# Half-width stationary values in the first attention stage of a fused attention and ELU feed-forward kernel

## The chip, the core and the metric

The kernel runs on one core of a Trainium2 chip. The metric is device time in microseconds (us). A core has TensorE (PE: matrix products into PSUM), VectorE (DVE), ScalarE (ACT), GpSimd (POOL) and SyncE (SP), which issues the DMAs. The engines run side by side, each through its own list of instructions in a fixed order, and wait for each other on semaphores.

## The reference

Eight batches of eight heads with 576 tokens and a head dimension of 64 go through causal attention with a decay bias, and the result, 4608 tokens of 512 values, through a feed-forward layer of 2048 with an ELU-like step between.

```python
scores = scale * np.matmul(q, k.transpose(0, 1, 3, 2))
cum = np.cumsum(np.maximum(s, 0.0), axis=-1)
bias = -(cum[:, :, :, None] - cum[:, :, None, :])
scores = np.where(causal, -1000000000.0, scores + np.minimum(bias, 0.0))
attn = np.exp(scores - np.max(scores, axis=-1, keepdims=True))
attn = attn / (np.sum(attn, axis=-1, keepdims=True) + 1e-09)
x = np.matmul(attn, v)            # then (B, S, H * D) as (4608, 512)
h = x @ w_in
g = np.where(h > 0.0, h, np.exp(np.minimum(h, 0.0)) - 1.0)
out = g @ w_out
```

## The kernel before, in words

The program first records operations (`op`), each with its engine or engines to choose from, an assumed cost, the tiles that it reads and writes, and a priority. `Plan.issue` then plays them through and writes them out: at each step it takes the operation that can start first by the assumed costs, so a changed cost or a changed operation may move anything that comes later, and may put a step on another engine. The instructions of an engine then run in exactly that order.

The attention is cut in two stages. The first stage (`Low`) takes the first 320 rows of batches 0, 1 and 2, twelve units of one batch and one pair of heads each, and works in plain fp32. The second stage (`Unit`) takes all the rest, in f16 parts. The feed-forward layer goes over 12 chunks of 384 tokens; chunk 0 runs in fp32 (`hidden_native`, L1313, and its `project`, L1358), the others in f16 parts (L1329, L1366). Chunk 0 needs the first stage's results of batches 0 and 1 and runs between its last units. Up to 60 us of the plan, PE gets filler transposes (L1429) where it would idle.

A unit of the first stage goes like this:

- `prepare_low` loads keys and queries of both heads (`kl`, `ql`) and the values (`vs`, two buffers in turn), and takes the largest magnitude of the values (`peak`, L579). The loaded block has seven slots of 64 columns: slot 0 with the first 64 keys' values of both heads, one above the other in the partitions, then for key blocks 0, 1 and 2 one slot for each head. `vs` keeps each slot with 64 columns of zeros beside it, so the DMA writes seven pieces a partition, 64 columns each and 128 apart. The zeros are written once, by four memsets in `zeros` (L511, L512).
- `scoring_low` makes the scores (L981), the masked row minimum (L984), exp (L989) and the normalized probabilities (L1002, L1004, L1006): one block for the pair's first 64 rows, and for each head blocks of 192 and 320 keys.
- `weighing_low` turns the probabilities with PE transposes (L793, L807) into `trl`, copies them to `tl` in SBUF (L417 on ACT or L418 on DVE), and multiplies with the values into one PSUM bank, `avl` (L788). `av` has one buffer, so a unit's first product waits until the last unit's results have been copied out.

The products are the step that changes. `own(k)` is a window of 128 stationary columns: a head's 64 value columns and 64 zeros, to the right of them for the first head and to the left for the second. So every product writes all 128 partitions of the bank; head 0 adds its values to partitions 0 to 63 and zeros to 64 to 127, head 1 the other way round. Key block 0 has 256 moving columns a head, block 1 has 192, block 2 has 64, and the pair's product has 128: seven fp32 products a unit, 84 in all. They accumulate in one group from the first (block 0, head 0, `start`) to the last (block 2, head 1, `stop`). Each is an operation of its own with the assumed cost `pe4(c)`.

The second stage's products (`heads`, L1143) already use 64 stationary columns a head, in f16, the two heads in turn, each into its own half of the bank's partitions.

Of the kernel before, what the change touches and what calls it, by code (L numbers as in the profile page):

```python
# [9 lines left out]
F32 = mybir.dt.float32  # L10
# [7 lines left out]
P = 128  # L18
# [25 lines left out]
N_CUT, CUT = 3, 2  # L44
# [241 lines left out]
def pe4(n):  # L286

    return 4 * pe(n)
# [41 lines left out]
def kernel(  # L330
# [26 lines left out]
    D = vb.shape[4]  # L357
    NP = H // 2
# [3 lines left out]
    HB = P // 2  # L362
    NQ = (S - HB) // P
# [4 lines left out]
    const = ctx.enter_context(tc.tile_pool(name="const", bufs=1))  # L368
# [8 lines left out]
    def load(prio, dst, src, reads, writes, nbytes, late=(), lag=LAG):  # L377
        return op(prio, [("SP", SP_COST, lambda: nc.sync.dma_start(dst(), src()), lag, nbytes)],
                  reads, writes, late)
# [53 lines left out]
    WM = S - P  # L433
    LOW = HB + CUT * P

    vs = [plan.buf(const, [P, NQ, 4, D], F32, f"vs_{k}") for k in range(2)]
    maskw = plan.buf(const, [P, WM], BF16, "maskw")
    masks = plan.buf(const, [P, 2, HB], BF16, "masks")

# [60 lines left out]
    def ones():  # L500

        for q, k in ((q2s, k2s), *zip(q2, k2)):
# [2 lines left out]
                pool.memset(k.v[HB:].bitcast(F32), 0.0)  # L505

            op(20, [("Pool-M", 700.0, rows)], [], [(q, "ones"), (k, ("aux", 0)), (k, ("aux", 1))])

    def zeros():
        for v in vs:  # L510
            op(-8, [("Pool-M", 450.0, lambda v=v: pool.memset(v.v[:, :, 3], 0.0))], [], [(v, "zeros")])  # L511
            op(-8, [("Pool-M", 100.0, lambda v=v: pool.memset(v.v[:, 0, 1], 0.0))], [], [(v, 1)])  # L512

    def mask_tiles():
        def whole():
# [191 lines left out]
    def prepare_low(u):  # L707

        b, j, prio = u.b, u.j, u.prio
        u.vs = vs[u.turn]  # L710
        u.k, clear = (k_first, None) if (b, j) == (0, 0) else low_keys(u.tag)
        u.q = plan.buf(sb, [P, 2 * LOW], F32, f"ql_{u.tag}", tag="qs", bufs=2)
        heads, h0 = slice(2 * j, 2 * j + 2), b * H + 2 * j
        at = slice(HB, HB + 1)
        load(prio, lambda: u.k.v[:HB], lambda: kT[b, :HB, heads, :LOW], [], [(u.k, "k")], P * LOW * 4)
        load(prio, lambda: u.q.v[:HB], lambda: qT[b, j, :HB, : 2 * LOW], [], [(u.q, "q")], P * LOW * 4)
        op(prio if b or j else -10, [("Pool-M", pool_1(2 * LOW), lambda: pool.memset(u.q.v[HB:], 1.0))],
           [], [(u.q, "ones")])
        if (b, j) > (0, 0):
            op(prio, clear, [], [(u.k, "sums")])  # L720

            src = aux if (b, j) == (0, 1) else aux_dram
            o = load(prio, lambda: u.k.v[at],
                     lambda: src.v[h0 : h0 + 2, 0, :LOW],
                     [(src, 0)], [(u.k, "sums")], 2 * LOW * 4)
        if (b, j) == (0, 1):
            urgent.append(o)
        n = 1 + 2 * (1 + CUT)

        def values():  # L730
            v = u.vs.v.rearrange("p n a d -> p (n a d)")[:, : n * P]
            return v.rearrange("p (n t d) -> p n t d", t=2, d=D)[:, :, 0]


        load(prio, values, lambda: vb[b, j, :, :n], [], [(u.vs, 0), (u.vs, 2)], P * n * D * 4)
        peak(prio, n * D, values, [(u.vs, 0), (u.vs, 2)], A_LOW + b * NP + j, mybir.AxisListType.XY)

    def scoring_low(u):
        prio = u.prio
# [37 lines left out]
    def weighing_low(u):  # L777
# [3 lines left out]
        av = plan.buf(ps, [P, 512], F32, f"avl_{u.tag}", tag="av", bufs=N_AV)  # L781
        ends = [P]

        def own(k):
            return u.vs.v.rearrange("p n a d -> p (n a d)")[:, k * HB : k * HB + P]

        def product(cost, k, src, dst, start, stop, reads):
            op(prio, [("PE", cost, lambda: pe_.matmul(av.v[:, dst], own(k), src(), start=start, stop=stop))],  # L788
               reads + [u.vs], [av])

        def pair():
            tr = plan.buf(ps, [P, 512], F32, f"trl_{u.tag}", tag="a", bufs=N_A)
            op(prio, [("PE", 111.0, lambda: pe_.transpose(tr.v[:, :P], u.first.v, ident))], [u.first], [tr])  # L793
            psum_copy(prio, P, lambda: turned.v[:, :P], lambda: tr.v[:, :P], [tr], [(turned, "pair")])
            product(pe4(P), 0, lambda: turned.v[:, :P], slice(n, n + P), True, True, [(turned, "pair")])

        def keys(kb):

# [14 lines left out]
            def dst():  # L813
                return turned.v[:, at : at + 2 * c].rearrange("p (h q) -> p h q", h=2)
# [1 line left out]
            psum_copy(prio, 2 * c, dst,  # L816
                      lambda: tr.v[:, : 2 * m * P].rearrange("p (h q) -> p h q", h=2)[:, :, m * P - c :],
                      [tr], [(turned, kb)])
            for h in range(2):
                product(pe4(c), 2 + 4 * kb + h, lambda h=h: dst()[:, h], slice(n - c, n),  # L820
                        kb == 0 and h == 0, kb == CUT and h == 1, [(turned, kb)])
            if kb < CUT:
                return
            key = u.b, u.j, False
# [606 lines left out]

    fillers()
    decay_sums()
    zeros()
    mask_tiles()
    for i in range(NQ):
        zero_pad(-9, pp[i], i)
# [99 lines left out]
```

## Time and profile before

| | |
|---|---|
| median of 3 runs | 1068.13 us (1066.83 to 1070.27) |
| the profiled execution | 1074.05 us |
| its span, from the first to the last instruction | 1072.3 us |
| busy PE / DVE / ACT / POOL | 1027.8 / 864.2 / 644.9 / 421.2 us |
| products of the first stage (L788) | 168 records, 16.9 to 105.3 us |
| products of the second stage (L1143) | 896 records, 147.4 to 938.3 us |

PE in the profile is the stream of products; PEld is the loading of stationary operands, which runs beside it. A group's busy time counts overlaps of its own instructions once. A product's recorded length goes from its start to the modelled end of its results, and the next one starts before that; what a product costs PE is the distance to the next start. An fp32 product shows as two records.

### The profile page before, as it was taken

Reading aid. Unit: us, or ns where it says so; the run is one execution under the profiler, and the core shown is the slowest. Engines: PE = TensorE matmul, PEld = TensorE weight load, DVE = VectorE, ACT = ScalarE, POOL = GpSimd, SP = SyncE. Lnnn points to the kernel's source line nnn. Section 1 sums busy time; section 2 is a strip of 40 time slices with the busy share of each in tenths; the row PEclk is TensorE's granted clock in tenths of the full one; section 3 lists DMA queues with packets and bytes.
Section 4 is the critical chain, followed back from the end, with each engine's and each line's share of the span. In section 5 each row is a group of like instructions: output and inputs, shape, how many; then the busy total and the mean of one; then the engine's idle time right before and its main releaser. Section 6 shows DMA issues by size and latency. Waiting matters only on the chain. (4 is left out here: it accounts for less than half of the span.)

```text
span 1072.3 us, 19689 instructions
## 1 busy us (share of the span) xinstructions
PE 1027.8 (96%) x6007; PEld 614.3 (57%) x6007; DVE 864.2 (81%) x2234; ACT 644.9 (60%) x1521; POOL 421.2 (39%) x649
## 2 busy tenths in 40 slices
PE   8889999899999999999999999999999999999998
PEld 7777555455555555555555555555555555555554
DVE  7788999999978988999898889898988888733433
ACT  5778675556666656566666666665566555544443
POOL 5532335433353445545543545444434534100000
PEclk9999999999999999999999999999999999999999
DMA  6788895536577666675577576757676557320000
GB/s 191 187 240 236 208 225 159 151 85 145 134 178 173 148 157 152 158 183 142 132 183 183 130 192 145 199 150 168 157 169 146 138 148 145 76 65 1 30 1 30
DMA packets 304313, 156.52 MB, mean 146 GB/s; under 512 B 224952, under 2 KB 278992, under 8 KB 304208
## 3 DMA queue, kind: packets, MB, share of 16 engines
q1 hardware_dynamic: 304208, 155.27, 59.2%
q8 instruction: 48, 0.79, 0.3%
q14 instruction: 57, 0.47, 0.1%
HBM read 79.66 MB, written 19.32 MB: 92 GB/s over the span
## 5 line engine op out<-in xcount | busy, mean ns | idle before, releaser
L1329 PE MATMUL h<-xh,wp 128*128 128x384 f16 x1408 | 392.7, 327 | 13.4 <-DVE gg L1347 11.7
L1366 PE MATMUL o<-wp,gg 128*128 128x512 f16 x1584 | 387.5, 380 | 0.0
L1329 PEld LDWEIGHTS <-wp 128*128 128x128 f16 x2112 | 197.2, 98 | 164.2 <-issue 23.4
L1366 PEld LDWEIGHTS <-gg 128*128 128x128 f16 x1584 | 146.4, 98 | 152.8 <-issue 5.4
L1329 PE MATMUL h<-xl,wp 128*128 128x384 f16 x704 | 229.6, 326 | 1.0 <-DVE xl L1282 0.9
L1293 ACT ACTIVATE g<-h,cs 128x384 f32<-128x384 f32 x176 | 101.8, 579 | 152.6 <-PE h L1329 150.7
L1042 DVE SCALAR_TENSOR_TENSOR p<-p,sm,p 128x512 f16<-128x512 f32 (+3 forms) x248 | 173.5, 723 | 7.3 <-POOL p L1034 5.3
L989 ACT ACTIVATE p<-p,mn 128x192 f32<-128x192 f32 (+1 forms) x232 | 144.0, 621 | 56.0 <-DVE mn L984 53.0
L1338 DVE SCALAR_TENSOR_TENSOR h<-g,cs,h 128x384 f32<-128x384 f32 x176 | 108.5, 616 | 74.7 <-ACT g L1300 73.4
L1034 POOL TENSOR_SCALAR p<-p,sm 128x512 f16<-128x512 f32 (+3 forms) x125 | 81.4, 658 | 137.2 <-DVE sm L995 42.0
L1342 ACT ACTIVATE gg<-h 128x384 f16<-128x384 f32 x160 | 78.0, 488 | 88.8 <-DVE h L1338 86.7
L981 PE MATMUL sc<-kh,qs 128*128 128x192 f32 (+2 forms) x272 | 118.8, 439 | 9.1 <-DVE mn L984 8.8
L984 DVE CUSTOM_DVE_ANT_0 p<-sc,maskw 128x192 f32<-128x192 f32 (+1 forms) x232 | 109.1, 480 | 15.8 <-PE sc L981 11.2
L1347 DVE SCALAR_TENSOR_TENSOR gg<-h,gg 128x384 f16<-128x384 f32 x176 | 97.1, 552 | 24.6 <-ACT gg L1342 22.6
L981 PE MATMUL sc<-k,q 128*128 128x192 f32 (+2 forms) x272 | 83.8, 311 | 0.2 <-DMA q<-qs 0.2
L981 PEld LDWEIGHTS sc<-kh,qs 128*128 128x128 f32 x272 | 51.7, 190 | 37.3 <-DVE mn L984 16.0
L1300 ACT ACTIVATE g<-g 128x384 f32<-128x384 f32 x132 | 68.9, 522 | 3.6
L411 POOL TENSOR_TENSOR k<-stk,kh 64x576 fp32r<-64x576 f32 x41 | 61.8, 1508 | 19.1 <-ACT kh L392 13.6
L1038 ACT ACTIVATE p<-p,sm 128x512 f16<-128x512 f32 (+3 forms) x98 | 56.7, 597 | 11.3 <-DVE sm L995 3.7
L1143 PE MATMUL av<-T,v 128*64 128x256 f16 (+5 forms) x896 | 61.0, 286 | 0.0
L1143 PEld LDWEIGHTS <-v 128*64 128x64 f16 x896 | 45.8, 110 | 23.0 <-issue 10.3
L402 POOL TENSOR_SCALAR xh<-xc,cs 128x384 f16<-128x384 f32 x32 | 21.6, 681 | 95.0 <-PE h L1329 89.7
(175 smaller groups left out, 1441.6 us busy)
## 6 DMA issues: line engine op xcount, KB each, us to landing
stk<-in_kT_dram SPq DMA_DIRECT2D x64, 288.0 KB
va<-in_vb_dram SPq DMA_DIRECT2D x32, 320.0 KB
stq<-in_qT_dram SPq DMA_DIRECT2D x40, 256.0 KB
w_i<-in_w_in_dram SPq DMA_DIRECT2D x16, 512.0 KB
w_o<-in_w_out_dram SPq DMA_DIRECT2D x16, 512.0 KB
out_dram<-ost SPq DMA_DIRECT2D x32, 256.0 KB
x_dram<-x_None SPq DMA_DIRECT2D x20, 288.0 KB
q<-qs SPq DMA_DIRECT2D x40, 128.0 KB
```

The costliest lines, as they stand in the source:

```text
L981: pe_.matmul(view(sc.v[:, :cw]), l, r, start=n == 0, stop=n == len(pairs) - 1)
L984: op(prio, [("DVE", 84 + dve_p(cw), lambda i=i, sc=sc: dve.tensor_tensor_reduce(pt.v[:, i * cw : (i + 1) * cw], sc.v[:, :cw], mv(i * cw, c ...
L989: op(prio, [("ACT", 480 + w / 1.2, lambda: act.activation(pt.v[:, :w], pt.v[:, :w], AF.Exp, bias=mn.v[:, n - 1 : n], scale=-1.0, accum_out ...
L1034: ("Pool", 160 + 1.04 * n, lambda part=part: pool.tensor_scalar(part(t16, 0), own(part), sm.v[:, r], 1.0, ALU.mult, ALU.mult)),
L1042: ("DVE-SB", dve_2(n), lambda part=part: dve.scalar_tensor_tensor(part(t16, 1), own(part), sm.v[:, r], part(t16, 0), ALU.mult, ALU.subtract)),
L1143: pe_.matmul(av.v[w.h * HB : (w.h + 1) * HB, dst], w.values.v[:, w.h, kb, v], part(w, kb, m), start=kb == 0 and m == 0 and v == 0, stop=kb ...
L1293: op(side, [("ACT", act_c(TC) + (0 if native else 90), lambda: act.activation(g.v[:, :TC], hp.v[:, :TC], AF.Exp, scale=1.0 if native else ...
L1329: pe_.matmul(hp.v[:, :TC], weight_part(f, 0, part)[1]()[:, c * P : (c + 1) * P], xx.v[:, c, :TC], start=(c == 0 and m == 0), stop=(c == NC ...
L1338: op(side, [("DVE", dve_p(TC), lambda: dve.scalar_tensor_tensor(hp.v[:, :TC], g.v[:, :TC], by(2 if sign[0] else 1), hp.v[:, :TC], ALU.mult ...
L1342: ("ACT", act_c(TC), lambda: act.activation(gg.v[:, 0, :TC], hp.v[:, :TC], AF.Copy, scale=2.0**-DOWN)),
L1347: op(side, [("DVE", dve_p(TC), lambda: dve.scalar_tensor_tensor(gg.v[:, 1, :TC], hp.v[:, :TC], 2.0**-DOWN, gg.v[:, 0, :TC], ALU.mult, ALU. ...
L1366: pe_.matmul(acc[i].v, gg.v[:, g, tb], weight_part(f, 1, part)[1](), start=(f == 0 and m == 0), stop=(f == NF - 1 and m == 2),)
```

## The change

The values are kept without zeros: `vs` is seven slots of 64 columns next to each other, `zeros` is gone with its four memsets, and the DMA writes one piece a partition. A product takes a head's 64 columns alone as its stationary operand and writes only that head's half of the bank's partitions: head 0 to partitions 0 to 63, head 1 to 64 to 127, which puts it in the other half of PE's columns. Each half now has its own accumulation group, from block 0 to block 2. Both heads' products of a key block are one operation, with the assumed cost of one (`pe4(c)` instead of twice that), one after the other in the list.

```diff
-    vs = [plan.buf(const, [P, NQ, 4, D], F32, f"vs_{k}") for k in range(2)]
+    n_low = 1 + 2 * (1 + CUT)
+    vs = [plan.buf(const, [P, n_low, D], F32, f"vs_{k}") for k in range(2)]
...
-    def zeros():
-        for v in vs:
-            op(-8, [("Pool-M", 450.0, lambda v=v: pool.memset(v.v[:, :, 3], 0.0))], [], [(v, "zeros")])
-            op(-8, [("Pool-M", 100.0, lambda v=v: pool.memset(v.v[:, 0, 1], 0.0))], [], [(v, 1)])
...
-        load(prio, values, lambda: vb[b, j, :, :n], [], [(u.vs, 0), (u.vs, 2)], P * n * D * 4)
-        peak(prio, n * D, values, [(u.vs, 0), (u.vs, 2)], A_LOW + b * NP + j, mybir.AxisListType.XY)
+        load(prio, lambda: u.vs.v, lambda: vb[b, j, :, :n_low], [], [u.vs], P * n_low * D * 4)
+        peak(prio, n_low * D, lambda: u.vs.v, [u.vs], A_LOW + b * NP + j, mybir.AxisListType.XY)
...
-        def own(k):
-            return u.vs.v.rearrange("p n a d -> p (n a d)")[:, k * HB : k * HB + P]
-
-        def product(cost, k, src, dst, start, stop, reads):
-            op(prio, [("PE", cost, lambda: pe_.matmul(av.v[:, dst], own(k), src(), start=start, stop=stop))],
-               reads + [u.vs], [av])
...
-            product(pe4(P), 0, lambda: turned.v[:, :P], slice(n, n + P), True, True, [(turned, "pair")])
+            op(prio, [("PE", pe4(P), lambda: pe_.matmul(
+                av.v[:HB, n : n + P], u.vs.v[:, 0], turned.v[:, :P], start=True, stop=True))],
+               [(turned, "pair"), u.vs], [av])
...
-            for h in range(2):
-                product(pe4(c), 2 + 4 * kb + h, lambda h=h: dst()[:, h], slice(n - c, n),
-                        kb == 0 and h == 0, kb == CUT and h == 1, [(turned, kb)])
+
+            def products():
+                for h in range(2):
+                    pe_.matmul(av.v[h * HB : (h + 1) * HB, n - c : n], u.vs.v[:, 1 + 2 * kb + h], dst()[:, h],
+                               start=kb == 0, stop=kb == CUT)
+
+            op(prio, [("PE", pe4(c), products)], [(turned, kb), u.vs], [av])
```

The plan then orders everything anew. Two places show it. PE, the fifth unit of the first stage (batch 1, heads 0 and 1), before; `trl` are its transposes (of `p` and `pl`, the probabilities), `avl` its products, `sc` the scores of later units, and the size at the end is that of the output (partitions by columns):

```order
L807 MATMUL trl_0_1_724<-ident,pl_1_0_598 128x128
L807 MATMUL trl_0_1_724<-ident,pl_1_0_612 128x128
L981 MATMUL sc_1_4_0_733<-kl_1_511,ql_1_517 128x320
L788 MATMUL avl_0_740<-tl_0_702,vs_90 128x128
L788 MATMUL avl_0_740<-tl_0_702,vs_90 128x256 x2
L788 MATMUL avl_0_740<-tl_0_702,vs_90 128x192 x2
L807 MATMUL trl_0_2_762<-ident,p_84 128x128
L807 MATMUL trl_0_2_762<-ident,pl_1_0_612 128x128
L981 MATMUL sc_2_0_0_765<-kl_2_567,ql_2_576 128x128
L981 MATMUL sc_2_1_0_772<-kl_2_567,ql_2_576 128x192
L788 MATMUL avl_0_740<-tl_0_702,vs_90 128x64 x2
```

The same unit on PE in the changed kernel, where the products stand in lines 777 (the pair's) and 806, and scores in 969:

```order
L777 MATMUL avl_0_713<-tl_0_703,vs_103 64x128
L791 MATMUL trl_0_1_717<-ident,p_82 128x128
L791 MATMUL trl_0_1_717<-ident,p_84 128x128
L791 MATMUL trl_0_1_717<-ident,pl_1_0_548 128x128
L791 MATMUL trl_0_1_717<-ident,pl_1_0_575 128x128
L969 MATMUL sc_2_2_0_723<-kl_2_585,ql_2_591 128x192
L806 MATMUL avl_0_713<-tl_0_703,vs_103 64x256 x2
L791 MATMUL trl_0_2_733<-ident,p_84 128x128
L791 MATMUL trl_0_2_733<-ident,pl_1_0_575 128x128
L969 MATMUL sc_2_3_0_738<-kl_2_585,ql_2_591 128x320
L806 MATMUL avl_0_713<-tl_0_703,vs_103 64x192 x2
L806 MATMUL avl_0_713<-tl_0_703,vs_103 64x64 x2
```

The seven products stood in two runs with other work between, and now stand in three. Over the twelve units the 84 products stood in 30 runs and now stand in 38: the pair's product is alone in twelve of them; eight units have their blocks 0 and 1 in one run (one of them with block 2 too), four have them apart, and block 2 is mostly alone.

POOL at the start of the program, before:

```order
L542 MEMSET p_87 128x64
L511 MEMSET vs_90 128x4x64
L717 MEMSET ql_0_94 64x640
L512 MEMSET vs_90 128x64
L511 MEMSET vs_107 128x4x64
L512 MEMSET vs_107 128x64
L570 MEMSET peaks 128x87
```

And in the changed kernel, at the same place; `masks` and `maskw` are the causal masks, which the first score blocks' VectorE steps read:

```order
L538 MEMSET p_87 128x64
L519 MEMSET masks 128x128
L521 AFFINE_SELECT masks<-masks 128x128
L525 MEMSET masks 64x64
L713 MEMSET ql_0_98 64x640
L512 MEMSET maskw 128x448
L513 AFFINE_SELECT maskw<-maskw 128x128
L566 MEMSET peaks 128x87
```

The four memsets of `vs` are gone, and the masks have moved ahead into their place.

More of the change, by code (lines that the diff above doesn't have):

```diff
@@ L727, in prepare_low @@
             urgent.append(o)
[L728 to L732, printed above, removed]
-        load(prio, values, lambda: vb[b, j, :, :n], [], [(u.vs, 0), (u.vs, 2)], P * n * D * 4)
-        peak(prio, n * D, values, [(u.vs, 0), (u.vs, 2)], A_LOW + b * NP + j, mybir.AxisListType.XY)
+        load(prio, lambda: u.vs.v, lambda: vb[b, j, :, :n_low], [], [u.vs], P * n_low * D * 4)
+        peak(prio, n_low * D, lambda: u.vs.v, [u.vs], A_LOW + b * NP + j, mybir.AxisListType.XY)
     def scoring_low(u):
@@ L1433 @@
     decay_sums()
-    zeros()
     mask_tiles()
```

## The prediction

> **What bounds the kernel now.** The page comes first, for the span and the busiest engine.
>
> ```profile
> span 1072.3 us, 19689 instructions
> PE 1027.8 (96%) x6007; PEld 614.3 (57%) x6007; DVE 864.2 (81%) x2234; ACT 644.9 (60%) x1521; POOL 421.2 (39%) x649
> ```
>
> TensorE (PE) is busy for 96% of the span, so its work sets the time wherever it isn't waiting. The busy time of each engine by stretch says where that is; the columns are the stretch, its length, then busy us of PE, PEld, DVE, ACT and POOL, the granted clock, the DMA share and GB/s.
>
> ```profile
> 0.00:10.00 10.00, 7.95 (x44) 7.58 (x45) 6.56 (x12) 1.78 (x3) 8.86 (x37) 1.00 0.69 165
> 30.00:40.00 10.00, 6.34 (x30) 4.57 (x29) 7.19 (x27) 7.29 (x23) 4.21 (x7) 0.87 0.88 228
> 40.00:50.00 10.00, 9.59 (x66) 8.67 (x65) 8.96 (x33) 8.19 (x27) 6.56 (x15) 0.96 0.46 129
> 60.00:70.00 10.00, 7.51 (x41) 5.51 (x40) 8.05 (x32) 7.24 (x23) 4.15 (x9) 1.00 0.85 250
> 80.00:90.00 10.00, 9.88 (x59) 8.44 (x58) 8.23 (x29) 8.72 (x28) 2.04 (x8) 1.00 0.94 239
> 100.00:110.00 10.00, 10.00 (x43) 6.54 (x42) 8.39 (x20) 6.17 (x16) 2.44 (x5) 1.00 0.85 252
> 300.00:400.00 100.00, 97.19 (x604) 56.78 (x602) 86.90 (x230) 61.41 (x147) 46.20 (x71) 1.00 0.67 162
> ```
>
> The products that change lie in the first 106 us. PE is nearly full at 40 to 50, 80 to 90 and from 100 on, and has holes at 30 to 40 and 60 to 70. Work that PE gains or loses there is mostly felt at the end, since later stretches are 97% full and can't absorb it. I count three quarters of it, because 30 to 40 and 60 to 70, with 6.34 and 7.51 of 10 us, would take some of it for nothing.
>
> **The products as they are.** The rows of the tile avl, then pieces of PE in order of time (start, length, what):
>
> ```profile
> L788 PEld LDWEIGHTS avl<-tl,vs x168: 186/190/337, 16.8 to 105.2; 128*128 128x128 f32 x168
> L788 PE MATMUL avl<-tl,vs x168: 219/326/483, 16.9 to 105.3; 128*128 128x256 f32 x48, 128*128 128x192 f32 x48, 128*128 128x64 f32 x48, 128*128 128x128 f32 x24
>   DVE tl L418: 7.1, 9
>   ACT tl L417: 2.3, 5
> ```
>
> ```profile
> 16.91 0.39 PE L788 MATMUL avl<-tl,vs 128*128 128x128 f32 x2
> 17.13 0.38 PE L807 MATMUL trl<-ident,p 128*128 128x128 f32 x2
> ...
> 19.09 1.68 PE L788 MATMUL avl<-tl,vs 128*128 128x256 f32 x8
> 20.60 0.27 PE L807 MATMUL trl<-ident,p 128*128 128x128 f32 x1
> ...
> 49.03 0.56 PE L788 MATMUL avl<-tl,vs 128*128 128x64 f32 x4
> 49.42 0.39 PE L807 MATMUL trl<-ident,p 128*128 128x128 f32 x2
> ```
>
> There are 84 products and 168 records: an fp32 product runs as two passes, each with a weight load. Recorded lengths overlap, so I take start to next start. The pair block's product costs 17.13 - 16.91 = 0.22 us; key blocks 0 and 1 (two heads of 256 columns, two of 192) cost 20.60 - 19.09 = 1.51 for 1792 columns in all passes, 0.84 ns a column; key block 2 costs 0.39. A unit costs 2.12, twelve units 25.4 us.
>
> **Do two halves overlap?** No fp32 product with 64 stationary columns is in this trace, but the second stage's f16 products have them, each head in its own half. One such run, its form, and its last weight loads:
>
> ```profile
> 328.25 0.33 PE L1329 MATMUL h<-xl,wp 128*128 128x384 f16 x1
> 328.42 0.33 PE L1329 MATMUL h<-xh,wp 128*128 128x384 f16 x1
> 328.67 2.12 PE L1143 MATMUL av<-T,v 128*64 128x512 f16 x28
> 330.73 0.40 PE L981 MATMUL sc<-kh,qs 128*128 128x288 f32 x1
> 330.96 0.30 PE L981 MATMUL sc<-k,q 128*128 128x288 f32 x1
> 331.10 0.25 PE L981 MATMUL sc<-kh,qs 128*128 128x192 f32 x1
> ```
>
> ```profile
> L1143 PE MATMUL av<-T,v x28: 193/299/403, 328.7 to 330.6; 128*64 128x512 f16 x6, 128*64 128x448 f16 x6, 128*64 128x320 f16 x6, 128*64 128x192 f16 x6
> ```
>
> ```profile
> 330.49 0.20 PEld L1143 LDWEIGHTS <-v 128*64 128x64 f16 x4
> 330.72 0.19 PEld L981 LDWEIGHTS sc<-kh,qs 128*128 128x128 f32 x1
> ```
>
> The 28 have 6 x (512 + 448 + 320 + 192) + 4 x 64 = 9088 columns. The full-width rows ahead of them go 384 columns in about 0.165 us, 0.43 ns a column, so one after another they would take 3.9 us. They took 330.73 - 328.67 = 2.06. So the two halves overlap almost wholly: 9088 / 2 x 0.43 = 1.95.
>
> They also show the price of going from full to half width and back. In: the run should begin at 328.42 + 0.165 = 328.585 and begins at 328.67, 0.09 late. Out: 2.06 - 1.95 = 0.11 passes beyond the stream, and the first full-width fp32 operand after it isn't loaded ahead: 330.73 to 330.96 is 0.23 where the next step with the same 288 columns is 0.14, 0.09 more. One run costs 0.29; with the first fp32 load of the run itself exposed, I take 0.30. A round trip costs 0.20 at the least (leaving out the late load) and about 0.37 at most (with a whole 0.19 load, less what is counted, at the run's start).
>
> **The sum.** The heads aren't interleaved by pass: each fp32 product issues both its passes, so the order is A1 A2 B1 B2. A1 and A2 share a half and run in turn, B1 starts with A2, and B2 runs alone or beside the next block's A1. At 0.84 ns a column, blocks 0 and 1 together take three steps of 256 and two of 192, 3 x 0.215 + 2 x 0.161 = 0.97 instead of 1.51. Block 2 is held by loads: four f16 half loads at (0.20 - 0.11) / 3 = 0.03 apart, twice that for fp32, gives 0.24 instead of 0.39 (between 0.16, three bare steps, and 0.39, no gain). The pair product stays 0.22, since one head block has nothing beside it. A unit saves 2.12 - 1.43 = 0.69, twelve 8.3. Four units lose 0.16 each, since the new order puts their blocks 0 and 1 apart. Saved: 7.7 us.
>
> Against it stand the switches. In the order of after the 84 products stand in 38 runs with full-width work on both sides, so 38 x 0.30 = 11.4. Before a wait for a turned copy (9 + 5 above) the way in is hidden, 14 x 0.09 = 1.3. Left: 10.1. PE has 10.1 - 7.7 = 2.4 us more, three quarters of it felt: +1.8.
>
> The Trainium skill says that changing the tiling mode, not just the tile, drains TensorE (TensorEngine Tiling (Array Packing), Key Properties). The run above agrees that there is a gap. If each switch had to wait out a whole recorded tail, 0.33 less 0.165 at the way in by the rows, the way in would be 0.165 instead of 0.09 and by that rule, an estimate, PE's sum would be nearly 3 us higher; the measured 0.09 decides.
>
> **Loads and memsets.**
>
> ```profile
> L378 SPq DMA_DIRECT2D vs<-in_vb_dram x12: 379/400/588, 3.5 to 92.3; - x12
> L511 POOL MEMSET vs<- x2: 318/418/519, 2.2 to 3.3; 128x256 f32 x2
> L512 POOL MEMSET vs<- x2: 147/265/383, 3.3 to 3.8; 128x64 f32 x2
>   DMA vs<-in_vb_dram: 5.8, 5
> ```
>
> ```profile
> DVE p L984 <- POOL maskw L517: 0.6, 1, 0.6
> ```
>
> The four memsets take at most 2 x 0.42 + 2 x 0.27 = 1.4 us of POOL, which works ahead of others there; the one wait for it is maskw's 0.6, so removing them gives 0 to 0.6. Values land in one piece of 1792 B a partition instead of seven of 256 B. VectorE's peaks waited 5.8 us in all for them, off PE's path where others were late too (30 to 40: DMA share 0.88). That gives nothing to a few us; nearest is the 0.6 of a direct wait. I take -0.5 for both. SP issues as many DMAs as before, and the wider reads of peaks have the same 448 elements. The second head's product no longer has a semaphore step of its own; it follows the first at once, so nothing new is queued behind a wait.
>
> The profiled execution took 1074.05 us, 1.75 more than its span, and lies 0.55% above the median of the runs. The sum there is 1074.05 + 1.8 - 0.5 = 1075.35; against the median, 1068.13 + 1.3 = **1069.4**. A measurement of this kernel can tell about 0.3%, 3.2 us.
>
> **The rivals.** *One after another* (0.25). No row shows fp32 halves beside each other. If fp32 passes take the way that both halves use, only block 2's loads get shorter: 12 x 0.15 = 1.8 saved against 10.1 of switches, +8.3 on PE, +6.2 felt, -0.5: 1073.8, slower. It decides as soon as the second head starts when the first has ended. For it: the two-step price of an fp32 column, 0.84 against 0.43. Against it: the f16 run.
>
> *Cheap switches* (0.20). PE waits 9.4 us in all ahead of these products; if stage one is held by the softmax chain as often as by PE, most switches fall into waits. The point is 7.7 / 38 = 0.20 a run; at 0.10, the way in alone, PE has 38 x 0.10 - 7.7 = 3.9 us less, 2.9 felt, and with 1.5 for loads and memsets it is 4.4 faster: 1063.7.
>
> *Everything halves* (0.03). If both passes of both heads run side by side and no switch costs anything, twelve units save half of 25.4, 12.7, three quarters felt, -9.5: 1058.6. The Trainium skill's span model for small packed products says about that: one product's time plus some ns a tile (TensorE: Matmul & The Clock Gate, Measured speedup vs the span model). The f16 run agrees on the overlap; the gaps around it disagree on the free switch.
>
> *PE doesn't matter here* (0.07). The change does nothing on the path, since stage one is held by loads; only the 0.5 is left: 1067.6.
>
> **How the numbers follow.** The forecast has 0.45. Its own range is 1066 to 1073, from a round trip at 0.20 to 0.37 (-1.4 to +5.1 on PE, -1.0 to +3.8 felt) and from the plan, which orders every later instruction anew and which I can't price from the trace. Within 0.3% is 1064.9 to 1071.3: the forecast gives 0.30 to that, 0.12 to slower and 0.03 to faster; one after another 0.22 slower and 0.03 same; cheap switches 0.13 faster and 0.07 same; everything halves 0.03 faster; the last one 0.06 same and 0.01 faster. In all faster 0.20, same 0.46, slower 0.34. The range, 1062 to 1077, leaves out everything halves, the lower end of cheap switches, and the worst plans.
>
> **What would show it.** Right: start to start, blocks 0 and 1 take about 0.97 us, with a record of one head starting within some ns of one of the other; a gap of about 0.1 on both sides of each run, and a first full-width step that is longer by 0.1. Wrong: blocks 0 and 1 still take 1.5 us (one after another), or no gaps beside the runs (cheap switches). If PE's work up to 106 us is as computed and the time differs by over 3 us all the same, the step that failed is that the plan's new order costs nothing.

## The result, and the profile after

The changed kernel took 1076.39 us (median of 12 runs, 1073.51 to 1080.8); the kernel before, run between them, 1070.44 us (12 runs, 1066.83 to 1074.33). The ratio is 1.0059, with a 95% interval from 1.0041 to 1.0077: slower by 6.3 us (6.0 between the medians). The forecast was 1069.4 us, that is 1.3 above the median known then, with a range from 1062 to 1077. The measured time lies in that range, 0.6 us below its upper end, and above the 1066 to 1073 that the prediction gave as the forecast's own range. The profiled execution took 1077.88 us, its span is 1076.1 us and its mean granted clock 0.990; before it was 1074.05, 1072.3 and 0.995.

**The products did what the change says, and more cheaply than forecast.** First the timeline of PE in the changed kernel, the first unit, at the places that the prediction showed of before (start, length, engine, line, what):

```profile
15.89 0.82 PE L969 MATMUL sc<-kl,ql 128*128 128x192 f32 x4
16.64 0.43 PE L777 MATMUL avl<-tl,vs 128*64 128x128 f32 x2
17.00 0.44 PE L791 MATMUL trl<-ident,p 128*128 128x128 f32 x2
17.27 0.38 PE L791 MATMUL trl<-ident,pl 128*128 128x128 f32 x2
...
18.47 0.70 PE L969 MATMUL sc<-kl,ql 128*128 128x320 f32 x2
19.10 0.98 PE L806 MATMUL avl<-tl,vs 128*64 128x256 f32 x8
20.01 0.33 PE L791 MATMUL trl<-ident,p 128*128 128x128 f32 x1
20.18 0.27 PE L791 MATMUL trl<-ident,pl 128*128 128x128 f32 x1
```

Key blocks 0 and 1 take 20.01 - 19.10 = 0.91 us, way out included, where they took 1.51; the pair's product takes 17.00 - 16.64 = 0.36 instead of 0.22. The rows of the tile avl in two short stretches show why the blocks are so fast (count, durations in ns, first and last start):

```profile
L806 PE MATMUL avl<-tl,vs x2: 430/430/430, 19.1 to 19.1; 128*64 128x256 f32 x2
L806 PE MATMUL avl<-tl,vs x4: 379/404/430, 19.1 to 19.4; 128*64 128x256 f32 x4
```

The first row is the stretch from 19.0 to 19.3, the second the one from 19.3 to 19.5, which counts the records that reach into it. Two records start together at 19.1 and two at 19.37, one of each head: in the trace the starts of a pair lie 7 ns apart. So both heads go through the same pass side by side. The pass order is A1 B1, A2 B2, and not A1 A2 B1 B2 as the prediction had it.

**The first stage ended earlier.** Its last product starts at 102.6 us, where it was 105.3. Busy us of PE, PEld, DVE, ACT and POOL by stretch in the changed kernel, then granted clock, DMA share and GB/s:

```profile
30.00:40.00 10.00, 8.61 (x56) 5.82 (x55) 7.90 (x35) 7.73 (x28) 5.95 (x13) 1.00 0.84 254
60.00:70.00 10.00, 9.47 (x58) 5.60 (x58) 8.73 (x33) 8.15 (x28) 5.01 (x11) 1.00 0.89 262
110.00:310.00 200.00, 185.40 (x893) 103.08 (x893) 175.63 (x430) 121.30 (x280) 87.75 (x127) 0.96 0.65 160
310.00:930.00 620.00, 601.19 (x3764) 353.56 (x3762) 543.28 (x1405) 380.14 (x880) 301.64 (x429) 1.00 0.67 158
```

The holes at 30 to 40 and 60 to 70 have shrunk (6.34 and 7.51 us busy before). But from 110 to 310 PE is busy for 185.40 of 200 us and VectorE (DVE) for 175.63. In the kernel before these are 189.47 and 181.97:

```profile
110.00:310.00 200.00, 189.47 (x930) 107.57 (x929) 181.97 (x446) 122.65 (x285) 81.65 (x114) 0.99 0.65 160
310.00:930.00 620.00, 603.00 (x3770) 353.91 (x3769) 542.52 (x1411) 384.07 (x885) 288.64 (x403) 1.00 0.66 157
```

Past 310 these busy times hardly differ; that time is lost there all the same is seen further down. The feed-forward's first product of chunks 1, 2 and 3 on PE's timeline says the same as times, in the kernel before:

```profile
197.61 0.33 PE L1329 MATMUL h<-xh,wp 128*128 128x384 f16 x1
...
279.66 0.33 PE L1329 MATMUL h<-xh,wp 128*128 128x384 f16 x1
...
363.01 0.33 PE L1329 MATMUL h<-xh,wp 128*128 128x384 f16 x1
```

and in the changed kernel:

```profile
190.06 0.33 PE L1317 MATMUL h<-xh,wp 128*128 128x384 f16 x1
...
267.62 0.32 PE L1317 MATMUL h<-xh,wp 128*128 128x384 f16 x1 [0.64 <-DVE gg L1335]
...
367.72 0.33 PE L1317 MATMUL h<-xh,wp 128*128 128x384 f16 x1
```

The changed kernel is 7.5 us ahead at chunk 1, 12.0 ahead at chunk 2 and 4.7 behind at chunk 3. So some 17 us go between 267 and 368 (part of that is second-stage work done then instead of earlier). The timeline of PE there has a hole:

```profile
278.79 0.42 PE L969 MATMUL sc<-kh,qs 128*128 128x320 f32 x1
279.04 0.31 PE L969 MATMUL sc<-k,q 128*128 128x320 f32 x1
282.70 0.32 PE L1317 MATMUL h<-xh,wp 128*128 128x384 f16 x1 [3.35 <-ACT xh L403]
283.83 0.48 PE L1317 MATMUL h<-xl,wp 128*128 128x384 f16 x1 [0.81 <-DVE xl L1270]
```

The waiting product belongs to chunk 2, whose last 192 rows are batch 3's. SP's queue shows those results stored at 274.75 and read back at 279.43, with three other transfers between (one of them left out here):

```profile
274.75 0.38 SPq L378 DMA_DIRECT2D x_dram<-x_None  x1
...
278.20 0.24 SPq L378 DMA_DIRECT2D k<-aux_dram  x1
278.49 0.47 SPq L378 DMA_DIRECT2D q2s<-qs_None  x1
279.43 0.33 SPq L378 DMA_DIRECT2D xc<-x_dram  x1
```

And behind the hole the granted clock falls, in the changed kernel:

```profile
280.00:290.00 10.00, 4.46 (x13) 2.22 (x13) 9.70 (x27) 6.05 (x14) 2.73 (x5) 0.68 0.82 211
290.00:300.00 10.00, 10.00 (x47) 5.28 (x46) 8.30 (x22) 5.76 (x15) 5.12 (x6) 0.81 0.76 195
```

where the kernel before has this:

```profile
280.00:290.00 10.00, 8.01 (x45) 4.54 (x44) 9.32 (x26) 6.68 (x16) 3.04 (x4) 1.00 0.92 179
290.00:300.00 10.00, 8.97 (x49) 4.75 (x48) 7.60 (x24) 4.99 (x13) 3.47 (x6) 1.00 0.81 167
```

The Trainium skill has such a drop (TensorE: Matmul & The Clock Gate, What's actually happening): it gives the array half its clock after an idle window of about 3.4 us. The hole of 3.35 us, and a clock of 0.50 from 285 to 290, are close to that. A hole of 2.70 us, met below with 0.52 behind it, is shorter than that rule has it. Whether the drop is a cause or a sign is tried below.

### The profile page after: what moved, and what is told of

Read it like the earlier page. It is cut to its first block, busy times and chain, and to the rows that moved or that the text cites. A ratio compares the mean times of both kernels' runs of the same rounds, so it can differ in the third digit from the quotient of the medians.

```text
span 1076.1 us, 19708 instructions
## 1 busy us (share of the span) xinstructions
PE 1028.8 (96%) x6014; PEld 597.0 (55%) x6014; DVE 859.3 (80%) x2216; ACT 640.2 (59%) x1511; POOL 443.2 (41%) x687
## 4 chain that ended last, share of the span: by engine, by line
PE 70%; DVE 16%; issue 5%; DMA 4%; ACT 2%; POOL 2%; SPq 1%; DVEq 0%; POOLq 0%; ACTq 0%
PE o L1354 24%; PE h L1317 23%; PE sc L969 8%; PE av L1131 5%; DVE p L1030 4%; PE o L1346 3%; PE h L1301 2%; DVE xl L1270 2%; DVE h L1326 2%; DVE wp L659 1%; DVE gg L1335 1%; DVE p L972 1%; PE trl L791 1%; DMA T<-p 1%; DMA stq<-in_qT_dram 1%
## 5 line engine op out<-in xcount | busy, mean ns | idle before, releaser
L1030 DVE SCALAR_TENSOR_TENSOR p<-p,sm,p 128x512 f16<-128x512 f32 (+3 forms) x237 | 168.9, 736 | 3.2 <-POOL p L1022 1.1
L1330 ACT ACTIVATE gg<-h 128x384 f16<-128x384 f32 x155 | 75.4, 487 | 93.2 <-DVE h L1326 91.6
L1335 DVE SCALAR_TENSOR_TENSOR gg<-h,gg 128x384 f16<-128x384 f32 x176 | 96.9, 550 | 22.0 <-ACT gg L1330 19.3
L411 POOL TENSOR_TENSOR k<-stk,kh 64x576 fp32r<-64x576 f32 x49 | 73.1, 1492 | 24.4 <-ACT kh L392 19.9
L411 POOL TENSOR_TENSOR qs<-stq,qs 64x512 fp32r<-64x512 f32 (+1 forms) x46 | 52.4, 1139 | 34.0 <-ACT qs L392 23.5
L390 POOL TENSOR_SCALAR qs<-stq 128x256 fp32r<-128x256 f32 (+1 forms) x43 | 24.3, 566 | 88.8 <-PE sc L969 57.5
```

The source lines that it names most:

```text
L411: ("Pool", pool_2(n), lambda: pool.tensor_tensor(dst(), src(), hi(), ALU.subtract)),
L1030: ("DVE-SB", dve_2(n), lambda part=part: dve.scalar_tensor_tensor(part(t16, 1), own(part), sm.v[:, r], part(t16, 0), ALU.mult, ALU.subtract)),
L1335: op(side, [("DVE", dve_p(TC), lambda: dve.scalar_tensor_tensor(gg.v[:, 1, :TC], hp.v[:, :TC], 2.0**-DOWN, gg.v[:, 0, :TC], ALU.mult, ALU. ...
```

## The experiments

Two theories stood first. A: the plan's new order loses the time, and the half-width products are about neutral. B: the half-width products lose it, by their switches between half and full width.

**Half-width products in the order before.** The kernel before, with the products alone changed; zeros, memsets, loads and every assumed cost stay, so each engine's list keeps its order.

```diff
-            return u.vs.v.rearrange("p n a d -> p (n a d)")[:, k * HB : k * HB + P]
+            return u.vs.v.rearrange("p n a d -> p (n a d)")[:, k * P : k * P + D]
...
-            op(prio, [("PE", cost, lambda: pe_.matmul(av.v[:, dst], own(k), src(), start=start, stop=stop))],
+            op(prio, [("PE", cost, lambda: pe_.matmul(
+                av.v[h * HB : (h + 1) * HB, dst], own(k), src(), start=start, stop=stop))],
...
```

Each half has its own accumulation group, as in the changed kernel.

> Half-width products (head 0 in partitions 0 to 63, head 1 in 64 to 127) in the order of before on every engine; the zeros, their memsets and the loads in seven pieces stay, unread zeros and all. Theory A, the new order of the plan costs the time and the products themselves about nothing: ratio to before 0.996 to 1.002, 1066 to 1072 us, the product blocks 0 and 1 at 0.9 us instead of 1.5 and the gaps of switching around them. Theory B, the half-width products and their switches cost it: ratio 1.004 to 1.008, as the changed kernel, 1075 to 1079 us.

Measured: 1070.32 us, ratio 1.0005 (0.9987 to 1.0022). Its first f16 product on PE's timeline starts 1.8 us earlier than before (197.61):

```profile
195.79 0.33 PE L1330 MATMUL h<-xh,wp 128*128 128x384 f16 x1
```

So the products alone lose nothing, and B falls. They gain about 2 us at the end of the first stage (the last product starts at 103.1 instead of 105.3), of which the whole kernel shows nothing beyond its interval.

**Full-width products in the new order.** The changed kernel's order on every engine, with the zeros and 128 columns back (the memsets stand inside the masks' step on POOL).

```diff
-                    pe_.matmul(av.v[h * HB : (h + 1) * HB, n - c : n], u.vs.v[:, 1 + 2 * kb + h], dst()[:, h],
-                               start=kb == 0, stop=kb == CUT)
+                    pe_.matmul(av.v[:, n - c : n], own(2 + 4 * kb + h), dst()[:, h],
+                               start=kb == 0 and h == 0, stop=kb == CUT and h == 1)
...
```

> The order of the changed kernel on every engine, with full-width products and zeros as before (four more memsets on POOL at the start, and loads in seven pieces). Theory A: ratio to before 1.004 to 1.010, 1075 to 1081 us. Theory B: 0.997 to 1.003, 1067 to 1073 us.

Measured: 1077.43 us, 1.0077 (1.0061 to 1.0093). The order alone costs as much as the whole change. This kernel also prices the products exactly, since each run of them stands between the same neighbours as in the changed kernel. Its PE timeline, first unit:

```profile
16.73 0.82 PE L979 MATMUL sc<-kl,ql 128*128 128x192 f32 x4
17.38 0.38 PE L787 MATMUL avl<-tl,vs 128*128 128x128 f32 x2
17.61 0.38 PE L801 MATMUL trl<-ident,p 128*128 128x128 f32 x2
17.82 0.38 PE L801 MATMUL trl<-ident,pl 128*128 128x128 f32 x2
...
19.02 0.70 PE L979 MATMUL sc<-kl,ql 128*128 128x320 f32 x2
19.56 1.68 PE L816 MATMUL avl<-tl,vs 128*128 128x256 f32 x8
21.07 0.27 PE L801 MATMUL trl<-ident,p 128*128 128x128 f32 x1
21.18 0.27 PE L801 MATMUL trl<-ident,pl 128*128 128x128 f32 x1
```

From the scores ahead to the second step behind, the pair's run takes 17.82 - 16.73 = 1.09 here and 17.27 - 15.89 = 1.38 in the changed kernel: +0.29, all of it the round trip to half width and back. It is spread over the way in (0.75 instead of 0.65), the run (0.36 instead of 0.23) and the first transposes behind (0.27 instead of 0.21). Blocks 0 and 1 take 21.18 - 19.02 = 2.16 here and 20.18 - 18.47 = 1.71 there: -0.45. With about 0.30 for the trip, as on the pair, the stream of 1.51 halves (-0.75).

Read this way from the two traces, the 38 runs give: 12 pairs at +0.29 = +3.5; 7 runs of blocks 0 and 1 at -0.455 = -3.2; 4 of block 0 alone at -0.13 = -0.5; 3 of block 1 alone at +0.02 = +0.1; 10 of block 2 alone at +0.015 = +0.15; one of blocks 1 and 2, -0.25; one of all three, -0.74. Sum: -1.0 us.

**Only the assumed cost.** The kernel before with all its products, and the plan's cost of the key blocks' products halved.

```diff
-                product(pe4(c), 2 + 4 * kb + h, lambda h=h: dst()[:, h], slice(n - c, n),
+                product(pe4(c) / 2, 2 + 4 * kb + h, lambda h=h: dst()[:, h], slice(n - c, n),
```

> The kernel before with nothing changed but the cost that the plan assumes for a key block's product, halved; the work on every engine is that of before, its order and the share of each engine differ. Theory A: the order alone moves the time by several us, either way, ratio below 0.997 or above 1.003 and the difference made after 150 us. Theory B: ratio within 0.997 to 1.003.

Measured: 1076.95 us, 1.0073 (1.0055 to 1.0092). One number in the plan, with no instruction changed in kind, costs what the change costs. This order is another one than the changed kernel's, and it too has PE waiting and a low clock between 280 and 300 (the stretch, then the longest wait from 190 to 310; total, times, longest):

```profile
280.00:300.00 20.00, 13.52 (x57) 6.70 (x56) 18.80 (x46) 10.97 (x26) 10.18 (x12) 0.74 0.75 186
PE h L1329 <- DVE gg L1347: 7.0, 4, 3.1
```

Here PE waits for the feed-forward's own `gg` on VectorE (3.06 us, up to 292.35) and for row minima (2.14, up to 283.86), not for rows of batch 3.

**The change with the old cost.** The changed kernel, and its step of two products counted at twice `pe4(c)`, which is what the two were counted before.

```diff
-            op(prio, [("PE", pe4(c), products)], [(turned, kb), u.vs], [av])
+            op(prio, [("PE", 2 * pe4(c), products)], [(turned, kb), u.vs], [av])
```

> The changed kernel with the cost that the plan assumes for a key block's pair of products doubled, which is the sum it assumed before. The products are half-width. Theory A: a different order, so a different time, anywhere from 0.996 to 1.010 of before, and by the products alone nearer to before than the changed kernel is. Theory B: the time of the changed kernel, 1.004 to 1.008.

Measured: 1067.87 us, 0.998 (0.9961 to 0.9999). All of the change's instructions are in it, and it is slightly faster than the kernel before. With the three runs above this settles A against B. The expectation took the order to be a new one, but it is nearly the order before: read in order of start, 44 of PE's 6007 rows stand in another place than in the kernel before, 18 of VectorE's 2234 and 2 of ScalarE's 1521. By the same reading 18 of PE's rows differ between the kernel before and the first experiment, which keeps its order; in the changed kernel 5099, 1997 and 1380 do. So of the whole change it is the assumed cost that moves the plan, and this run is a second one in the old order, not a new order that is good.

**The cost raised.** Is every order but the old one slow? The kernel before, with that cost at 1.25 times.

```diff
-                product(pe4(c), 2 + 4 * kb + h, lambda h=h: dst()[:, h], slice(n - c, n),
+                product(1.25 * pe4(c), 2 + 4 * kb + h, lambda h=h: dst()[:, h], slice(n - c, n),
```

> The kernel before, only the assumed cost of the key blocks' products raised by a quarter instead of halved, so that the plan orders everything anew in the other direction: before the second, third and fourth step of the second stage's products PE has 108, 159 and 231 of the feed-forward's f16 products behind it, where it has 126, 177 and 252 in the order before, 144, 201 and 252 in the changed kernel's and 135, 192 and 243 in the order of the run with halved cost. Theory R (the new order loses because the feed-forward runs ahead of the batches that it needs): no hole over 2.7 us in PE from 200 to 300, ratio 0.997 to 1.002. Theory P (the order before is a good one among many; any reordering of the 20,000 instructions loses about as much, in whatever place): ratio 1.003 to 1.009, with the loss in other places than 260 to 310.

Measured: 1068.76 us, 0.9987 (0.9966 to 1.0008). The longest hole of PE from 200 to 300 is 0.98 us. Its stretch from 110 to 310, which stands against 185.40 and 175.63 in the changed kernel:

```profile
110.00:310.00 200.00, 190.88 (x945) 108.75 (x944) 181.09 (x453) 123.61 (x292) 98.74 (x132) 1.00 0.65 161
```

So P falls: this order is as new as the others (4885 of PE's rows stand in another place than before), its feed-forward doesn't run ahead, and it costs nothing. That fits R. It is one such order against two that lose, so R is borne out and not proved; the next runs try it further.

**Chunk 2 without batch 3.** The changed kernel, with the last rows of chunk 2 read from batch 0 (their output is then made from other data), and the same edit on the kernel before.

```diff
-                     lambda c=c, b=b, r=r, n=n: x_dram.v[b, c, :, r : r + n],
+                     lambda c=c, b=0 if (ch, b) == (2, N_CUT) else b, r=r, n=n: x_dram.v[b, c, :, r : r + n],
```

> The changed kernel in the changed kernel's own order, except that the feed-forward chunk 2 reads its last 192 rows from batch 0's results, long stored, and not from batch 3's: the output for those 192 rows is made from other data. Theory A1 (the loss arises because chunk 2 runs ahead of the batch that it needs, PE stands still for about 3.4 us at 279 to 283, and the granted clock falls behind it): the hole at 280 shrinks to under 1 us, the clock from 280 to 300 is back above 0.95 where it was 0.68 and 0.81, and the ratio to the kernel before falls from 1.006 to 1.000 to 1.003. Theory A2 (the new order loses by small losses everywhere, the hole is one of many signs): hole gone or not, the ratio stays at 1.004 to 1.008.

> The kernel before with the same single edit (chunk 2's last 192 rows read from batch 0's results, so their output is made from other data), as a control. In its order nothing waits for batch 3 there, so both theories expect the ratio within 0.998 to 1.002 and no hole in PE from 270 to 300. If it is faster by more than that, the wait cost the kernel before something too and the gain of the experiment on the changed kernel has to be read against it.

Measured: 1075.54 us, 1.0047 (1.0029 to 1.0065), and for the control 1070.39 us, 0.9999 (0.9979 to 1.0019). The control is as expected; its longest hole there, 1.44 us, is one that the kernel before has too. In the changed kernel A1 failed on its own sign: the hole shrank from 3.35 to 2.70 us only, and the clock fell all the same (0.52 from 280 to 290). The ratio is A2's. The rows of SP's queue in it:

```profile
277.00 0.24 SPq L378 DMA_DIRECT2D k<-aux_dram  x1
277.29 0.47 SPq L378 DMA_DIRECT2D q2s<-qs_None  x1
277.81 0.58 SPq L378 DMA_DIRECT2D xc<-x_dram  x1
```

The load now follows `q2s` without a wait of its own, so batch 3's store is no longer what it waits for. But it stands behind transfers of the second stage that come no earlier: `k` starts 10.58 us after the chunk's first product in both kernels. ScalarE shows one more link. Its step `xh`, which PE waits for, follows a second-stage step at once:

```profile
279.05 1.23 ACT L1026 ACTIVATE p<-p,sm 128x384 f16<-128x384 f32 x2 [0.62 <-ACT p L977]
280.19 0.60 ACT L403 ACTIVATE xh<-xc,cs 128x384 f16<-128x384 f32 x1
```

In the changed kernel it does so too (`p` at 280.92 for 1.23 us, `xh` at 282.05). So the wait for the data was one of several that end together, and this run can't say what the hole costs.

**The holes filled.** Are the hole and the clock behind it the loss? Useless products on PE keep it busy there: zeros times `xh`, added to sums that they leave as they are.

```diff
+    nil = const.tile([P, P], F16, name="nil")
+    dve.memset(nil, 0.0)
...
+                    for _ in range({(1, 4, 0): 15, (2, 1, 2): 17}.get((ch, f, c), 0)):
+                        pe_.matmul((hp if c else acc[0]).v[:, :TC], nil, xh.v[:, 0, :TC], start=False, stop=False)
```

> The changed kernel in its own order, with useless products (zeros times values that are there already, added to sums that they don't change) on PE just before the two products that PE waits longest for: 15 of 384 columns, 2.5 us, before the one at 209 and 17, 2.8 us, before the one at 282.7. Nothing else moves, and no wait of another engine ends earlier. Theory C (a good part of the loss is the granted clock, which falls behind each long hole of PE; over the timed runs the clock lost 10.4 us in the changed kernel and 4.8 in the kernel before): the clock at 205 to 215 and 280 to 300 is back above 0.95, the mean clock rises from 0.990 to 0.994 or more, the ratio falls from 1.006 to 1.001 to 1.003. Rival H (the loss is the time that PE waits there and elsewhere; the clock falls in stretches that wait anyway and costs nothing): ratio 1.005 to 1.008, whatever the clock does.

> The same with the 17 useless products before the one at 282.7 alone. Theory C: the clock at 280 to 300 is back above 0.95 and the one at 205 to 215 is not; of the time that the two fillings win together this one wins the larger part, ratio 1.002 to 1.004. Rival H: 1.005 to 1.008.

> A control, and a candidate for the fastest version: the kernel that counted twice the cost for the products (0.998), with 8, 9 and 10 useless products, 1.3 to 1.65 us, before the products that PE waits 1.8 to 2.1 us for at 213, 405 and 490. Its clock lost only 4.2 us over the timed runs, most of it before 45 us, so theory C expects 0 to 1.5 us from it, ratio 0.996 to 0.999. If useless products make any kernel faster by 4 us, the experiment on the changed kernel says nothing about its loss; rival H expects 0.998 to 1.000.

Measured: 1078.97 us, 1.0095 (1.006 to 1.0129) with both; 1077.28 us, 1.0081 (1.0055 to 1.0107) with the one; 1067.36 us, 0.9964 (0.9944 to 0.9985) for the control. The second filling came out one step of products ahead of the wait, and the hole is gone all the same. The filling of both, by stretch:

```profile
205.00:215.00 10.00, 8.65 (x49) 4.69 (x48) 9.78 (x18) 4.62 (x9) 0.00 (x0) 1.00 0.90 200
280.00:300.00 20.00, 17.13 (x83) 9.60 (x83) 17.02 (x51) 12.79 (x33) 8.95 (x11) 0.91 0.90 202
110.00:310.00 200.00, 189.53 (x945) 106.41 (x944) 178.19 (x441) 122.77 (x284) 92.74 (x131) 0.99 0.68 164
310.00:930.00 620.00, 597.92 (x3732) 350.36 (x3730) 538.37 (x1392) 378.41 (x872) 300.66 (x422) 0.99 0.68 157
```

The clock came back: 1.00 and 0.91 there (C had asked for 0.95), and over the timed runs the clock (one less the granted share, times the span) lost 5.9 us, where it lost 10.4 in the changed kernel and 4.3 in the kernel before. The time did not come back. Chunk 3 starts at 362.52, 5.2 us ahead of the changed kernel and 0.5 ahead of the kernel before (363.01), and chunk 8 at 789.58 against 789.01 in the changed kernel:

```profile
362.52 0.33 PE L1321 MATMUL h<-xh,wp 128*128 128x384 f16 x1
...
789.58 0.33 PE L1321 MATMUL h<-xh,wp 128*128 128x384 f16 x1
```

So theory C falls for the kernel as a whole. H fits better, though both ratios (1.0095 and 1.0081) lie just above its range and only their intervals reach into it: between chunk 1 (188.84, already 1.2 us ahead of the changed kernel) and chunk 3 the filling won some 4 us, and in the end nothing. What PE gained early it gave back between 360 and 790 (597.92 busy us from 310 to 930, where the changed kernel has 601.19), so this order loses time there too, and not by the clock at 280. The control lies where C had it, at the lower edge, and is not faster by 4 us; so the useless products by themselves neither slow a kernel nor speed it up by what is in question. It is the fastest of all versions, ahead of both kernels, but its interval overlaps that of the version without them (0.9961 to 0.9999).

**Fewer trips.** The kernel before in its order, with half width in blocks 0 and 1 alone; and the same in the order of the run with doubled cost.

```diff
+                if kb == CUT:
+                    wide_product(pe4(c), 2 + 4 * kb + h, lambda h=h: dst()[:, h], slice(n - c, n),
+                                 False, h == 1, [(turned, kb)])
+                    continue
+                product(pe4(c), 1 + 2 * kb + h, h, lambda h=h: dst()[:, h], slice(n - c, n),
+                        kb == 0, False, [(turned, kb)])
...
```

> The kernel before in its own order, with only key blocks 0 and 1 on half-width stationary columns; the pair's product and block 2 stay full width. Where all products were half width in this order (30 runs of them) the ratio was 1.0005. Theory S (every round trip between half and full width costs PE about 0.30 us, and the pair's product and block 2 hardly gain from half width): some 15 round trips fewer, 4.5 us less PE, against block 2's lost gain of 12 x 0.15 = 1.8 at most: 2.7 us less of PE in the first 106 us, the last product of the first stage some 1 to 2 us earlier than 103.05, ratio 0.996 to 1.000. Rival S0 (switches cost nothing to speak of): the last product is later by 1 to 2 us and the ratio 1.000 to 1.003.

> The order of the run that counted twice the cost for the products (ratio 0.998), with only key blocks 0 and 1 on half-width columns; pair and block 2 at full width, with the zeros, their memsets (in the masks' step on POOL) and the seven-piece loads back. Theory S: another 1 to 3 us less of PE in the first stage, ratio 0.995 to 0.998. Rival S0: 0.998 to 1.001, as the memsets and the loads in pieces come back for nothing. If the ratio is at 0.998 whatever the first stage gains, what is gained ahead of the batches is not kept later.

Measured: 1071.08 us, 0.9996 (0.9973 to 1.0019), and 1070.49 us, 0.9998 (0.9979 to 1.0018). The pair's product is back at 0.22 us in both, but the last product of the first stage starts at 106.2 us in the first, later than 103.05 and not earlier as S had it; in that execution the clock was at 0.79 and 0.87 from 70 to 80 us, where the run with all products at half width had 1.00. In the second it starts at 103.6, where the run with doubled cost has 102.9, again not earlier. Both intervals reach into S and S0, so the ratios decide nothing between them: two or three us of PE in the first stage are below what the whole kernel shows. As the order of the run with doubled cost is nearly the order before, the two are nearly the same program, and they agree.

## Where the prediction was right, and where it was wrong

The time fell into the range and the kernel got slower, as the forecast had it, but that was luck: the forecast was slower for more work on PE, and PE got less. The step that failed is the plan's order, taken at nothing.

- **Do two halves overlap?** Right, for fp32 too; *one after another*, the rival that had the kernel clearly slower, was wrong in its mechanism.
- **Blocks 0 and 1.** The step was mis-sized: 0.97 with A1 A2 B1 B2 taken for the order of passes, 0.76 measured (1.51 halved) with A1 B1 A2 B2. The 0.91 of the rows looks like the 0.97, but it has the way out in it. Block 2 was taken at 0.24 and came to 0.39 + 0.015 - 0.29, about 0.12.
- **The round trip.** Right: 0.30 forecast, 0.29 measured on the pair's product. The Trainium skill's rule that a change of tiling mode drains TensorE (TensorEngine Tiling (Array Packing), Key Properties) agrees with the gaps on both sides of each run.
- **The sum on PE.** Wrong in sign: +2.4 us forecast, -1.0 measured run by run in one and the same order, and 1.8 us won by the first f16 product in the order before. The switches cost about 38 x 0.29 = 11.0; the streams saved 12.0 where the forecast had 7.7.
- **Three quarters of it felt.** Neither borne out nor excluded: of the 1.8 us won by the first f16 product in the order before nothing is seen in the total (1.0005), but three quarters of it, 1.4 us, would be 0.9987, the lower end of the interval. The reason given, that later stretches are 97% full, was read from 300 to 400; from 200 to 300 PE was busy for 91.74 of 100 us.
- **Loads and memsets, -0.5.** Never run alone. The nearest pair is the run with doubled cost, which has the loads in one piece and no memsets, against the half-width products in the order before, which keep both: 1067.87 against 1070.32, with intervals that overlap. That fits a gain and doesn't show one.
- **The plan's new order.** This is the step that failed. The prediction could give it no price, took it at nothing in the sum and left it to the range, which for that reason just reached the result. It cost about 8 us in the two runs that change little else (1.0077 and 1.0073), and that is the whole result. The prediction's last sentence had named this step for the case that came.

Why does the order lose? Shown: it is the order, and it comes from the assumed cost. Shown too: neither the data of batch 3 nor the clock behind the two holes, taken alone, is the cause.

Where it loses can be read from the traces by work. Count the moving columns of all products on PE but the first stage's `avl`, the filler transposes and the useless ones, with half-width products at half; the total is the same in every kernel. The table says how much later (+) or earlier (-) than the kernel before a kernel has done as much as that one has at the time at the head, in us, from one profiled execution each.

| kernel | 190 | 280 | 300 | 550 | 750 | end |
|---|---|---|---|---|---|---|
| half-width products, order before | -1.7 | -1.7 | -1.8 | -1.4 | -3.5 | -4.4 |
| cost raised | +1.8 | -0.7 | -3.2 | -3.9 | -2.3 | -1.8 |
| the change | -9.2 | -5.5 | +2.5 | +0.2 | +6.6 | +3.8 |
| only the cost halved | -0.7 | -2.7 | +4.3 | +1.4 | +5.8 | +4.2 |
| the change, both holes filled | -10.4 | -8.7 | -2.4 | -2.2 | +6.7 | +4.7 |

The change and the halved cost lose 8.0 and 7.0 us between 280 and 300, and 6.4 and 4.4 again between 550 and 750, of which they win some back before and after. With the holes filled the kernel loses 6.3 between 280 and 300, is still ahead there, and loses 8.9 between 550 and 750. That is more than the 2 us by which two executions of one order drift apart there (first row). So there are two places at least, and the experiments looked at the earlier one alone.

Argued: told that the products cost half, the plan lets the feed-forward run ahead; the second stage's steps then come later beside it, and PE waits for what VectorE, ScalarE and the DMAs have yet to do. That the wait is for rows of a batch that is barely done holds for the changed kernel only; with the halved cost alone PE waits there for other things. The one other order without loss, with the cost raised, has no such hole. What loses the time between 550 and 750, and which of the plan's single decisions carries the loss, stays open.

## What to carry to other kernels

Where a planner or scheduler orders the program, an edit to an operation is two edits, the work and the cost in the plan; time them apart, by running the new work in the old order and the old work in the new order. An assumed cost that is nearer the truth can give a worse order. By `pe4` the key blocks' products of the twelve units count 32.4 us as before and 16.2 halved. At full width they take 22.8 (12 times 1.51 + 0.39), and at half width, trips and all, about 18.4, by the 26 runs above that aren't the pair's. Halving the count cost about 8 us; keeping the old one with the new products gave 0.998, and raising it, farther yet from the truth, cost nothing. And a hole with a low clock behind it is not yet a loss to be won back: filling it mended the clock and part of the delay up to there, and the kernel lost the time later.

## What the runs showed of the hardware

- Two fp32 products in the two column halves start 7 ns apart, pass by pass, and the next two 0.27 us later (19.10 and 19.37, the first step of the run), so a pair of heads takes half the time in the stream (1.51 to 0.76 us without the trip). The Trainium skill's span model for packed products has about 4 ns a tile (TensorE: Matmul & The Clock Gate, Measured speedup vs the span model), which is close.
- A trip from full to half width and back costs 0.29 us of PE around fp32 work, so a lone product of 128 columns gets dearer (0.22 to 0.51) and two times 64 columns break even.
- A hole of PE well below 3 us can be followed by a low clock, and the same hole need not be. In the kernel before, 2.64 us without a product, at 202 to 204, stand ahead of a clock of 0.85. In the run with doubled cost a hole of 2.64 us at the same step ends at 201.58, and the clock stays at 1.00 up to 220. With chunk 2 read from batch 0, 2.70 us stand ahead of 0.52 from 280 to 290. The rows are of the kernel before: the longest wait of PE for that step from 190 to 310 (total, times, longest), then the stretch.

```profile
PE sc L981 <- DVE mn L984: 3.0, 2, 2.6
```

```profile
205.00:215.00 10.00, 10.00 (x49) 5.70 (x48) 8.12 (x21) 6.25 (x14) 6.54 (x9) 0.85 0.40 108
```
